# Retention with a recurrent state and a GELU feed-forward on one core: odd batches' heads swapped for 64x64 quarters, q and k loaded by rows and transposed by DMA

## The chip, the core and the metric

The kernel runs on one core of one Trainium2 chip. The metric is the device time of one execution in microseconds (us). The engines are named as the profile names them: PE (TensorE, matmuls), PEld (its weight loads), DVE (VectorE), ACT (ScalarE), POOL (GpSimd) and SP (SyncE, which here only issues DMAs).

## What is computed

```python
batch, n_heads, seq, head_dim = (4, 8, 768, 64)
gamma = 1.0 - 2.0 ** (-5.0 - np.arange(H))
for t in range(S):
    state = gamma * state + einsum('bhd,bhe->bhde', k[:, :, t], v[:, :, t])
    y[:, :, t] = scale * einsum('bhd,bhde->bhe', q[:, :, t], state)
x = y.transpose(0, 2, 1, 3).reshape(B * S, H * D)
h = x @ w_in                       # 3072 x 512 times 512 x 2048
g = 0.5 * h * (1 + tanh(c * (h + 0.044715 * h**3)))
out = g @ w_out                    # 3072 x 2048 times 2048 x 512
```

q, k, v and the output are float32.

## The kernel before

The sequence is cut into six chunks of 128 tokens (NCk = 6), and a chunk holds 128 tokens of all four batches, 512 rows. Within a chunk and a batch the recurrence becomes matmuls, in fp16:

- Transposed q and k (tile `qkT`, 128 partitions = two heads of 64): with two heads side by side on the partitions, there are four head pairs, `hp`.
- Scores, `mm_A` (L247, matmuls on L252): for each head pair and each of its heads j, k times q over 64 partitions, a 128x128 result. `ev_A` (L261, DVE on L265) multiplies them by a mask.
- State times q, `mm_yc` (L268, matmuls on L276): for each head, the 64x64 state times q. Head j sits on partitions 64j to 64j+63 of both operands and writes the same partitions of the result, so the two heads use two of the array's four 64x64 quarters.
- Scores times v, `mm_yi` (L285, L289), added into the same PSUM bank; `ev_Y` (L298) takes the sum to `xT`, the feed-forward's input.
- The state's update, `mm_s` (L307, L313) and `ev_S` (L321, L330).

The feed-forward of a chunk has two phases. `moe1` (L416; `moe1_two`, L422, in halves) multiplies `xT` by `w_in` on L398 in 16 units of d_ff and applies GELU on ACT (L414). `units_w` (L518) multiplies by `w_out` in 14 units of eight matmuls (L536) over a scheme of seven products instead of eight, which needs sums of GELU's results (`g_sums`, L476, on POOL until the last chunk, L467), three snapshots of partial results on ACT (L559) and a last copy (L565).

The order of the work is written by hand. `run(units, after)` (L597) issues the units of one chunk's feed-forward, and behind unit i the steps listed in `after[i]`: the preparation and the attention matmuls of the next chunk, and the loads and preparation of the one after it. Every engine and every DMA queue takes its instructions in that order. [...]

How q and k get into `qkT` before the change:

- Chunks 0 and 1: rows are loaded (`load1`, L100: 128 tokens x 8 heads x 64, 256 KB, in runs of 256 bytes), cast or scaled to fp16 (`prep1`, L184), transposed on PE against an identity (`mm_T`, L222, L229) and copied out of PSUM (`ev_T`, L234).
- Chunks 2 to 5, q, and chunks 3 to 5, k: `load_blk` (L106, issued on L113) loads them in 16 DMAs of 64 KB each, in runs of 128 bytes, so that head pairs and halves of a head already lie on the partitions; `prep_blk` (L201, L204) casts them; and VectorE's stream transpose, which works on blocks of 32x32, finishes the transpose (L238). k is loaded a second time by rows, for the state's update. Chunk 2's k goes by way of PE's transposes.
- `load(c)` (L117) issues a chunk's loads: chunk 2's is called ahead of chunk 1's feed-forward (L733), chunk 3's behind unit 8 of it (L746), and chunk c+2's behind unit 0 of chunk c (L798).

The stage between chunk 1's two phases is written on L734 to L769: chunk 2's q and k are prepared on ACT behind units 8, 9, 10 and 11 of `moe1` and units 0 and 1 of `units_w(1)`, chunk 2's first scores (batches 0 and 1) stand behind unit 14 and the others behind unit 4 of `units_w(1)`. From chunk 2 on the loop on L772 does the same with other unit numbers: scores of batches 0 and 1 of the next chunk behind unit 12, state times q behind units 19 and 25.

Of the kernel before, what the change touches and what calls it, by code (L numbers as in the profile page):

```python
# [9 lines left out]
F16 = mybir.dt.float16  # L10
# [6 lines left out]
def kernel(  # L17
# [30 lines left out]
    cst_np = np.concatenate([qdec, kdec, gst, tri], axis=1).astype(np.float32)  # L48
# [17 lines left out]
    OQ, OK, OG, OT = 0, H, 2 * H, 2 * H + NHP  # L66
# [12 lines left out]
    BLK = {"q": (2, 3, 4, 5), "k": (3, 4, 5)}  # L79

    def ld_all(key):
        if key not in raw:
            raw[key] = ld.tile(
                [128, B * NHP, 4, 32],
                F32,
                tag=key[0],
                bufs=2 if key[0] == "q32" else 1,
                name=key[0],
            )
        return raw[key]  # L90

    def ld_tile(nm, c, b):
        if nm == "q":
            t = ld_all(("q32", c)).rearrange("p (b hp) a d -> p b (hp a d)", b=B)
            return t[:, b].rearrange("p (h d) -> p h d", h=H)
        if (nm, c, b) not in raw:
            raw[nm, c, b] = ld.tile([128, H, Dh], F32, tag=f"{nm}32", bufs=8, name=f"{nm}32")
        return raw[nm, c, b]
# [7 lines left out]
    def load_blk(nm, c):  # L106
        t = ld_all((nm + ("32" if nm == "q" else "T32"), c))
        src = srcs[nm].rearrange("b (hp j) s (dd d) -> j dd s (b hp) d", j=2, dd=2)
        for j in range(2):
            for dd in range(2):  # L110
                for a in range(4):
                    p0, t0 = (2 * j + dd) * 32, c * C + a * 32
                    nc.sync.dma_start(  # L113
                        out=t[p0:p0 + 32, :, a, :], in_=src[j, dd, t0:t0 + 32]
                    )

    def load(c):  # L117
        load_blk("q", c)
        if c in BLK["k"]:
            for b in range(B):  # L120
                load1(nc.sync, "v", c, b)
            load_blk("k", c)
            for b in range(B):
                load1(nc.sync, "k", c, b)
        else:
            for b in range(B):
                for nm in "kv":
                    load1(nc.sync, nm, c, b)
# [32 lines left out]
    st = const.tile([128, B, NHP, 64], F16, name="st")  # L161
# [14 lines left out]
    blk16 = {}  # L176
# [6 lines left out]

    def prep1(eng, nm, c, b):  # L184
        t = pre.tile(
            [128, H, Dh], F16, tag=f"{nm}16", bufs=6 if nm == "q" else 2 * B, name=f"{nm}16"
        )
        src = ld_tile(nm, c, b)
        if (nm == "v") == (c < 2):
            copy_on(eng, t, src)  # L190
        else:
            col = OQ if nm == "q" else OK
            eng.tensor_tensor(  # L193
                out=t,
                in0=src,
                in1=cst[:, col:col + H].unsqueeze(2).broadcast_to([128, H, Dh]),
                op=ALU.mult,
            )
        h16[nm, c, b] = t

    def prep_blk(eng, nm, c, b):  # L201
        key, tag = ("q32", "q16") if nm == "q" else ("kT32", "kT16")
        t = pre.tile([128, NHP * 4, 32], F16, tag=tag, bufs=6 if nm == "q" else B, name=tag)
        copy_on(  # L204
            eng, t, ld_all((key, c))[:, b * NHP:(b + 1) * NHP].rearrange("p hp a d -> p (hp a) d")
        )
        blk16[nm, c, b] = t
# [14 lines left out]
    def mm_T(c, b):  # L222
        parts = [(i, nm) for i, nm in enumerate("qk") if c not in BLK[nm]]
        if not parts:
            return
        ps = bank("att", F16, (128, 2, NHP, 128), "qkT_ps")
        for i, nm in parts:
            for hp in range(NHP):
                nc.tensor.transpose(  # L229
                    out=ps[:, i, hp], in_=pair(h16[nm, c, b], hp), identity=iden  # L230
                )
        pss["T", c, b] = ps

    def ev_T(c, b, eng=nc.vector):  # L234
        t = att.tile([128, 2, NHP, 128], F16, tag="qkT", name="qkT")
        for i, nm in enumerate("qk"):
            if c in BLK[nm]:
                nc.vector.transpose(  # L238
                    out=t[:, i].rearrange("p hp t -> p (hp t)"),
                    in_=blk16.pop((nm, c, b)).rearrange("p ha d -> p (ha d)"),  # L240
                )
        if ("T", c, b) in pss:
            i0 = sum(c in BLK[nm] for nm in "qk")
            copy_on(eng, t[:, i0:], pss.pop(("T", c, b))[:, i0:])
        qkT[c, b] = t

    def mm_A(c, b):  # L247
        t = qkT[c, b]
        ps = [bank("att", name=f"a_ps{j}") for j in range(2)]
        for hp in range(NHP):  # L250
            for j in range(2):
                nc.tensor.matmul(  # L252
                    out=ps[j][:, hp],
                    lhsT=t[j * 64:(j + 1) * 64, 1, hp],
                    rhs=t[j * 64:(j + 1) * 64, 0, hp],
                    start=True,
                    stop=True,
                )
        pss["A", c, b] = ps

    def ev_A(c, b):  # L261
        ps = pss.pop(("A", c, b))
        for j in range(2):
            s = att.tile([128, NHP, 128], F16, tag=f"a{j}", name=f"a_sb{j}")
            nc.vector.tensor_tensor(out=s, in0=ps[j], in1=mask[:, j], op=ALU.mult)  # L265
            a_sb[c, b, j] = s

    def mm_yc(c, b, tag):  # L268
        y_ps = pss["Y", c, b] = bank(tag, name="y_ps")
        if c == 0:  # L270
            return

        for hp in range(NHP):
            for j in range(2):
                sl = slice(j * 64, (j + 1) * 64)
                nc.tensor.matmul(  # L276
                    out=y_ps[sl, hp],
                    lhsT=st[sl, b, hp],
                    rhs=qkT[c, b][sl, 0, hp],
                    start=(hp == 0),  # L280
                    stop=False,
                    skip_group_check=True,
                )
# [23 lines left out]
    def mm_s(c, bs, tag="att"):  # L307
# [3 lines left out]
        for i, b in enumerate(bs):  # L311
            for h in range(H):
                nc.tensor.matmul(  # L313
                    out=s_ps[h % 2 * 64:(h % 2 + 1) * 64, i, h // 2],
                    lhsT=h16["k", c, b][:, h],
                    rhs=h16["v", c, b][:, h],
                    start=True,
                    stop=True,
                )

    def ev_S(c, bs, eng=nc.vector):  # L321
# [3 lines left out]
        t = st[:, bs[0]:bs[-1] + 1]  # L325
        if c == 0:
            copy_on(eng, t, s_ps)
            return
        for hp in range(NHP):
# [3 lines left out]
                scalar=cst[:, OG + hp:OG + hp + 1],  # L333
# [14 lines left out]
    def att_AY(c, bs, tag, ca, abs_, eng):  # L348


        for b in bs:
            mm_yc(c, b, tag)
# [272 lines left out]
    mm_yc(0, 0, "o")  # L625
# [19 lines left out]
    mm_yc(0, 1, "o")  # L645
# [19 lines left out]
    mm_yc(0, 2, "o")  # L665
# [7 lines left out]
    mm_yc(0, 3, "o")  # L673
# [24 lines left out]
    def preps(c, b):  # L698
        prep1(VE, "q", c, b)
        prep1(PO, "k", c, b)  # L700
        prep1(AC, "v", c, b)

# [35 lines left out]
            for fp in range(NF // 2)  # L738
# [7 lines left out]
            8: [(prep_blk, AC, "q", 2, 0), (load, 3)],  # L746
            9: [(prep1, AC, "k", 2, 0)],
            10: [(att_T, 2, 0), (prep_blk, AC, "q", 2, 1)],
            11: [(prep1, AC, "k", 2, 1), (g_sums, PO, 1, 0, 4, 1, 2)],
            12: [(att_T, 2, 1)],  # L750
# [7 lines left out]
            0: [(prep_blk, AC, "q", 2, 2), (prep1, AC, "k", 2, 2)],  # L758
            1: [(att_T, 2, 2), (prep_blk, AC, "q", 2, 3), (prep1, AC, "k", 2, 3)],
            2: [(att_T, 2, 3)],  # L760
            4: [(att_AY, 2, (0, 1), "h", 2, (2, 3), AC)],
            9: [(att_AY, 2, (2, 3), "h", 2, (), AC), (mm_s, 2, (0, 1)), (mm_s, 2, (2, 3)),
                (ev_S, 2, (0, 1)), (ev_S, 2, (2, 3))],
            10: [(prep_blk, AC, "q", 3, 0)] + [(prep1, PO, "v", 3, b) for b in range(B)],
            11: [(prep_blk, AC, "q", 3, 1)],
            12: [(prep_blk, AC, "q", 3, 2)],
            13: [(prep_blk, AC, "q", 3, 3)],
# [4 lines left out]
    for c in range(2, NCk):  # L772
# [3 lines left out]
            15: [(att_T, n, 3)],  # L776
            16: [(prep1, AC, "k", n, 0), (prep1, AC, "k", n, 1)],
            17: [(prep1, AC, "k", n, 2), (prep1, AC, "k", n, 3)],
            19: [(att_AY, n, (0, 1), "h", n, (2, 3), VE)],
            25: [(att_AY, n, (2, 3), "h", n, (), AC), (mm_s, n, (0, 1)), (mm_s, n, (2, 3)),  # L780
                 (ev_S, n, (0, 1)), (ev_S, n, (2, 3))],
# [5 lines left out]
        if n < NCk:  # L787
            for b in range(B - 1):
                if c == 2:
                    more((8, 9, 11)[b], (prep_blk, AC, "k", n, b))  # L790
                more(((9, 10, 13) if c == 2 else (6, 8, 13))[b], (att_T, n, b))
            if c == 2:
                more(13, (prep_blk, AC, "k", n, 3))
# [3 lines left out]
        if m < NCk:  # L797
            more(0, (load, m))  # L798
            for b in range(B):
                more((20, 21, 23, 24)[b], (prep_blk, AC, "q", m, b))  # L800
                more(24, (prep1, PO, "v", m, b))
                more(29, (prep_blk, PO, "k", m, b))
# [31 lines left out]
```

## Time and profile before

| | us |
|---|---|
| median of 3 runs | 212.22 |
| the three runs | 210.81, 212.77, 212.22 |
| the profiled execution's time | 210.97 |
| its span, first to last instruction | 209.2 |
| PE busy | 200.5 |
| scores, L252: 192 matmuls, busy | 8.1 |
| state times q, L276: 160 matmuls, busy | 6.7 |
| PE transposes, L229: 80 matmuls, busy | 7.8 |
| DVE stream transposes, L238: 28, busy | 19.3 |
| ACT's waits for the feed-forward's first matmuls | 34.0 |

A chunk of the middle takes some 30 us: chunk 2's `moe1` starts at 88.08 and chunk 3's at 118.79. How to read it: busy times of PE count matmuls that overlap, so the chain of work, in order of time, is the better view of what a group costs. The granted TensorE clock is 1.00 throughout. DMA is the busy share of the 16 DMA engines; between 58 and 68 us it is above 1.00 by the profile's count, at 221 to 242 GB/s.

### The profile page before, as it was taken

The numbers are of one execution on the slowest core, as the hardware profiler recorded it, in microseconds if no ns is written. First come the engines' busy times: TensorE is split into PE (matmuls) and PEld (weight loads), VectorE is DVE, ScalarE is ACT, GpSimd is POOL, SyncE is SP. The second block draws the span as 40 slices with busy tenths as digits, with TensorE's granted clock in tenths as the row PEclk, the third lists the DMA queues.
The fourth block names the chain that finished last, engine by engine and source line by source line (L and its number), as shares of the span: only waits on it lengthen the run. The fifth ranks groups of instructions, "written<-read, shape, count | busy, mean of one in ns | idle before, by whom it ended". The sixth has DMA issues, their size and how long they took to land.

```text
span 209.2 us, 4776 instructions
## 1 busy us (share of the span) xinstructions
PE 200.5 (96%) x1928; PEld 132.2 (63%) x1928; DVE 103.8 (50%) x213; ACT 102.0 (49%) x182; POOL 115.6 (55%) x120
## 2 busy tenths in 40 slices
PE   7889999999998999999999999999999999999992
PEld 2447744456786878844688744688644788545881
DVE  3445144478733647803855730865632684053430
ACT  2483563154449625178745266633365811566311
POOL 0596001133089999249999299997499980200000
PEclk9999999999999999999999999999999999999999
DMA  7999999998899688699888798797960000500004
GB/s 167 285 257 207 206 206 222 273 252 227 166 205 244 106 159 174 105 292 216 125 193 147 124 350 139 146 200 109 236 197 0 0 3 0 204 0 0 0 28 177
DMA packets 124438, 33.19 MB, mean 159 GB/s; under 512 B 117952, under 2 KB 122432, under 8 KB 124416
## 3 DMA queue, kind: packets, MB, share of 16 engines
q1 hardware_dynamic: 108272, 21.09, 50.5%
q0 software_dynamic: 5456, 8.65, 17.6%
q10 hardware_dynamic: 10688, 3.15, 6.4%
q8 instruction: 15, 0.25, 0.4%
q14 instruction: 7, 0.06, 0.1%
HBM read 30.78 MB, written 6.29 MB: 177 GB/s over the span
## 4 chain that ended last, share of the span: by engine, by line
PE 90%; ACT 4%; DMA 2%; issue 1%; ACTq 0%; SPq 0%; DVE 0%
PE h_ps L398 39%; PE o_ps L536 29%; PE o_ps L432 7%; PE a_ps L252 3%; PE y_ps L289 3%; PE y_ps L276 3%; PE qkT_ps L229 2%; DMA iden<-rr_ident 2%; PE s_ps L313 2%; PE spin_ps L156 1%; ACT g L414 1%; ACT qkT L180 1%; ACT k L180 1%; ACT q L180 1%; ACTq L101 0%
## 5 line engine op out<-in xcount | busy, mean ns | idle before, releaser
L398 PE MATMUL h_ps<-xT,w_in 128*128 128x512 f16 (+2 forms) x488 | 87.4, 334 | 0.5 <-ACT g L414 0.5
L414 ACT ACTIVATE g<-h_ps 128x512 f16<-128x512 f32 (+1 forms) x98 | 57.5, 589 | 34.3 <-PE h_ps L398 34.0
L398 PEld LDWEIGHTS <-w_in 128*128 128x128 f16 x488 | 45.4, 97 | 37.4 <-issue 2.8
L467 POOL TENSOR_TENSOR s_g<-g 128x512 f16<-128x512 f16 x32 | 37.0, 1155 | 9.3 <-ACT g L414 9.3
L265 DVE TENSOR_TENSOR a_sb<-a_ps,mask 128x512 f16<-128x512 f32 x48 | 30.1, 683 | 22.9 <-PE a_ps L252 22.9
L536 PEld LDWEIGHTS <-s_g 128*128 128x128 f16 x320 | 30.5, 98 | 4.3
L536 PE MATMUL o_ps<-t_w,s_g 128*128 128x256 f16 x240 | 27.3, 273 | 0.0
L536 PEld LDWEIGHTS <-g 128*128 128x128 f16 x240 | 23.4, 98 | 3.5
L467 POOL TENSOR_TENSOR s_g<-s_g,g 128x512 f16<-128x512 f16 x16 | 18.5, 1156 | 1.3
L536 PE MATMUL o_ps<-w_out,g 128*128 128x256 f16 x160 | 18.6, 273 | 0.0
L467 POOL TENSOR_TENSOR s_g<-g,s_g 128x512 f16<-128x512 f16 x16 | 18.5, 1156 | 0.0
L193 POOL TENSOR_TENSOR k<-k,cst 128x512 f16<-128x512 f32 x8 | 8.4, 1053 | 17.4 <-DMA k<-in_k_dram 17.4
L569 POOL DMA_DIRECT2D out_dram<-o_sb x8 | 5.9, 739 | 19.6 <-DVE o_sb L467 18.1
L193 POOL TENSOR_TENSOR v<-v,cst 128x512 f16<-128x512 f32 x16 | 16.2, 1044 | 0.0
L565 ACT COPY o_sb<-o_ps 128x512 f32<-128x512 f32 (+1 forms) x5 | 2.7, 543 | 25.3 <-PE o_ps L536 25.3
L432 PE MATMUL o_ps<-w_out,g 128*128 128x512 f16 x64 | 14.8, 379 | 0.0
L238 DVE STREAM_TRANSPOSE qkT<-kT 128x512 f16<-128x512 f16 x12 | 8.2, 679 | 12.9 <-ACT kT L180 8.9
L305 DVE TENSOR_TENSOR xT<-y_ps,dec 128x512 f16<-128x512 f32 x16 | 10.3, 686 | 4.5 <-PE y_ps L289 4.5
L238 DVE STREAM_TRANSPOSE qkT<-q 128x512 f16<-128x512 f16 x16 | 11.1, 691 | 2.6 <-ACT q L180 2.5
L559 ACT COPY s_u<-o_ps 128x512 f32<-128x512 f32 (+1 forms) x6 | 3.1, 515 | 17.4 <-PE o_ps L536 10.6
L156 PE MATMUL spin_ps<-zero 128*128 128x512 f16 x32 | 9.9, 447 | 1.2 <-DVE zero L148 1.2
L330 DVE SCALAR_TENSOR_TENSOR st<-st,cst,s_ps 128x128 f16<-128x128 f16 (+1 forms) x40 | 9.9, 315 | 2.0 <-PE s_ps L313 2.0
(55 smaller groups left out, 184.7 us busy)
## 6 DMA issues: line engine op xcount, KB each, us to landing
k<-in_k_dram SPq DMA_DIRECT2D x22, 256.0 KB, 4.3
v<-in_v_dram SPq DMA_DIRECT2D x18, 256.0 KB, 4.5
q<-in_q_dram SPq DMA_DIRECT2D x64, 64.0 KB, 2.9
out_dram<-o_sb POOLq DMA_DIRECT2D x8, 512.0 KB, 4.4
kT<-in_k_dram SPq DMA_DIRECT2D x48, 64.0 KB, 2.8
w_in<-in_moe_w_in_dram POOLq DMA_DIRECT2D x4, 512.0 KB, 8.9
w_out<-in_moe_w_out_dram POOLq DMA_DIRECT2D x4, 512.0 KB, 14.8
v<-in_v_dram ACTq DMA_DIRECT2D x6, 256.0 KB, 5.6
```

The costliest lines, as they stand in the source:

```text
L156: nc.tensor.matmul(out=ps, lhsT=zero[:, 0:128], rhs=zero, start=True, stop=True)
L180: eng.copy(out=out, in_=in_)
L193: eng.tensor_tensor(out=t, in0=src, in1=cst[:, col:col + H].unsqueeze(2).broadcast_to([128, H, Dh]), op=ALU.mult,)
L238: nc.vector.transpose(out=t[:, i].rearrange("p hp t -> p (hp t)"), in_=blk16.pop((nm, c, b)).rearrange("p ha d -> p (ha d)"),)
L265: nc.vector.tensor_tensor(out=s, in0=ps[j], in1=mask[:, j], op=ALU.mult)
L305: nc.vector.tensor_tensor(out=x, in0=ps, in1=dec, op=ALU.mult)
L330: nc.vector.scalar_tensor_tensor(out=t[:, :, hp], in0=t[:, :, hp], scalar=cst[:, OG + hp:OG + hp + 1], in1=s_ps[:, :, hp], op0=ALU.mult, o ...
L398: nc.tensor.matmul(out=out, lhsT=w_in_sb[wi][:, kc, wr * 128:(wr + 1) * 128], rhs=xT[c][:, kc, t0:t1], start=(kc == 0), stop=(kc == NHP - ...
L414: nc.scalar.activation(out=out, in_=in_, func=AF.Gelu_apprx_tanh, scale=1.0)
L432: nc.tensor.matmul(out=ps[:, n0:n1], lhsT=g_sb[c, fc // 8][:, fc % 8, b * C:(b + 1) * C], rhs=w_out_sb[fc // (NF // NO)][:, fc % (NF // NO ...
L467: eng.tensor_tensor(out=out, in0=in0, in1=in1, op=op)
L536: nc.tensor.matmul(out=po, lhsT=lhs(c, lk, fp, a), rhs=rhs(rk, fp), start=(new and fp == 0 and (last or a == 0)), stop=(stop and fp == NP ...
```

## The change

Four things are changed together.

1. In odd batches the two heads of each pair are swapped where q and k are prepared (`heads`), so head j sits on partitions of the other half. The state of odd batches is kept in that order too (`st` is split by parity, a second set of decay columns `gst_o`), `mm_s` takes v of the other head, and `ev_A` picks the other PSUM bank.
2. `mm_yc` takes the batches of a step together: for each head pair it issues two batches times two heads, and these four matmuls lie on the four 64x64 quarters of the array.
3. `mm_A` computes each 128x128 score in two halves of 64 rows: 16 matmuls of 64x64 weights per batch instead of 8 of 64x128.
4. Chunks 2 to 5 load q, k and v by rows only (`load`: twelve DMAs of 256 KB), cast q and k on ACT into one tile `qk16`, and one DMA on SP's queue, `dma_T`, transposes the tile (128 x 1024, fp16) into `qkT`. `load_blk`, `prep_blk`, the stream transposes and PE's transposes of chunk 2's k are gone. The preparation of chunk n moves into the `units_w` phase two chunks earlier in full; `qkT` has 6 buffers instead of 4.

The core of the diff:

```diff
     def load(c):
-        load_blk("q", c)
-        if c in BLK["k"]:
...
+        for b in range(B):
+            load1(nc.sync, "q", c, b)
+            load1(nc.sync, "k", c, b)
+        for b in range(B):
+            load1(nc.sync, "v", c, b)
...
+    def heads(ap, b):
+        v = ap.rearrange("p (hp j) d -> p hp j d", j=2)
+        return v[:, :, ::-1] if b % 2 else v
...
+    def dma_T(c, b):
+        nc.sync.dma_start_transpose(
+            out=qkT_tile(c, b).rearrange("p i hp t -> p (i hp) t"),
+            in_=qk16.pop((c, b)).rearrange("p i h d -> p (i h d)"),
+        )
...
     def mm_A(c, b):
         t = qkT[c, b]
         ps = [bank("att", name=f"a_ps{j}") for j in range(2)]
         for hp in range(NHP):
-            for j in range(2):
...
+            for m in range(2):
+                for j in range(2):
+                    nc.tensor.matmul(
+                        out=ps[j][m * 64:(m + 1) * 64, hp],
+                        lhsT=t[j * 64:(j + 1) * 64, 1, hp, m * 64:(m + 1) * 64],
+                        rhs=t[j * 64:(j + 1) * 64, 0, hp],
...
+    def mm_yc(c, bs, tag):
...
         for hp in range(NHP):
+            for b in bs:
+                for j in range(2):
+                    r = j ^ b % 2
+                    sl = slice(r * 64, (r + 1) * 64)
+                    nc.tensor.matmul(
+                        out=pss["Y", c, b][j * 64:(j + 1) * 64, hp],
+                        lhsT=st_of(b)[sl, hp],
+                        rhs=qkT[c, b][sl, 0, hp],
...
+    def preps2(c, b):
+        prep1(AC, "q", c, b)
+        prep1(AC, "k", c, b)
+        dma_T(c, b)
...
-            8: [(prep_blk, AC, "q", 2, 0), (load, 3)],
-            9: [(prep1, AC, "k", 2, 0)],
-            10: [(att_T, 2, 0), (prep_blk, AC, "q", 2, 1)],
-            11: [(prep1, AC, "k", 2, 1), (g_sums, PO, 1, 0, 4, 1, 2)],
-            12: [(att_T, 2, 1)],
+            8: [(prep1, AC, "q", 2, 0), (load, 3)],
+            9: [(prep1, AC, "k", 2, 0), (dma_T, 2, 0)],
+            10: [(prep1, AC, "q", 2, 1)],
+            11: [(prep1, AC, "k", 2, 1), (dma_T, 2, 1), (g_sums, PO, 1, 0, 4, 1, 2)],
...
-            0: [(prep_blk, AC, "q", 2, 2), (prep1, AC, "k", 2, 2)],
-            1: [(att_T, 2, 2), (prep_blk, AC, "q", 2, 3), (prep1, AC, "k", 2, 3)],
-            2: [(att_T, 2, 3)],
+            0: [(prep1, AC, "q", 2, 2), (prep1, AC, "k", 2, 2), (dma_T, 2, 2)],
+            1: [(prep1, AC, "q", 2, 3), (prep1, AC, "k", 2, 3), (dma_T, 2, 3)],
...
-            10: [(prep_blk, AC, "q", 3, 0)] + [(prep1, PO, "v", 3, b) for b in range(B)],
-            11: [(prep_blk, AC, "q", 3, 1)],
-            12: [(prep_blk, AC, "q", 3, 2)],
-            13: [(prep_blk, AC, "q", 3, 3)],
+            10: [(preps2, 3, 0)],
+            11: [(preps2, 3, 1)],
+            12: [(preps2, 3, 2)],
+            13: [(preps2, 3, 3)] + [(prep1, PO, "v", 3, b) for b in range(B)],
...
-            15: [(att_T, n, 3)],
-            16: [(prep1, AC, "k", n, 0), (prep1, AC, "k", n, 1)],
-            17: [(prep1, AC, "k", n, 2), (prep1, AC, "k", n, 3)],
...
-                more((20, 21, 23, 24)[b], (prep_blk, AC, "q", m, b))
+                more((20, 21, 23, 24)[b], (prep1, AC, "q", m, b))
+                more((21, 23, 24, 26)[b], (prep1, AC, "k", m, b), (dma_T, m, b))
                 more(24, (prep1, PO, "v", m, b))
-                more(29, (prep_blk, PO, "k", m, b))
```

## The prediction

> **What bounds the kernel now.** I read the page's busy shares and its chain of work first, then the chain in order of time around the places that the diff touches, then SyncE's own list of DMA issues, and last GpSimd's order in chunk 2.
>
> ```profile
> span 209.2 us, 4776 instructions
> PE 200.5 (96%) x1928; PEld 132.2 (63%) x1928; DVE 103.8 (50%) x213; ACT 102.0 (49%) x182; POOL 115.6 (55%) x120
> ...
> PE 90%; ACT 4%; DMA 2%; issue 1%; ACTq 0%; SPq 0%; DVE 0%
> ```
>
> TensorE is the bound: 90% of the chain is its matmuls. So what leaves VectorE, ScalarE or GpSimd gains nothing by itself; what counts is TensorE's instructions and whatever makes it wait.
>
> ```profile
> 64.38 0.51 ACT k L180
> 64.90 0.05 issue
> 64.94 0.40 PE qkT_ps L229 x4
> ...
> 69.55 0.55 PE a_ps L252 x16
> 70.11 0.98 PE h_ps L398 x8
> 71.09 1.76 PE o_ps L536 x16
> ...
> 76.69 0.56 PE y_ps L276 x16
> 77.26 0.55 PE a_ps L252 x16
> ...
> 88.08 11.69 PE h_ps L398 x52
> ...
> 145.06 0.51 PE s_ps L313 x32
> ```
>
> Columns: start, length, piece. To be seen: 16 matmuls of state times q (L276) and 16 of the scores (L252) cost 0.55 us each; the stage from 63 to 75 is the one where ScalarE's copies of q and k hold TensorE up; and 32 small matmuls of L313, each with its own weight load, take 0.51 us, 16 ns each.
>
> ```profile
> 46.48 1.50 SPq L732 DMA_DIRECT2D dec<-rr_dec  x1
> 48.07 9.48 SPq L113 DMA_DIRECT2D q<-in_q_dram  x16
> 57.59 0.49 SPq L101 DMA_DIRECT2D k<-in_k_dram  x1
> ...
> 65.03 10.06 SPq L113 DMA_DIRECT2D q<-in_q_dram  x16
> ...
> 133.07 3.12 SPq L101 DMA_DIRECT2D v<-in_v_dram  x4
> ```
>
> SyncE issues chunk 2's loads from 48.07 and goes straight on to chunk 3's at 65.03. It is never idle here: the DMA engines set its pace. The eight row loads (256 KB) from 57.59 to 65.03 took 7.44 us, 0.93 us each.
>
> ```profile
> k<-in_k_dram SPq DMA_DIRECT2D x22, 256.0 KB, 4.3
> out_dram<-o_sb ACTq DMA_DIRECT2D x2, 256.0 KB, 2.0
> ```
>
> From issue to landing, 256 KB took 4.3 us in the busy queue and 2.0 us (the last stores) in an idle one.
>
> **Part 1: chunk 2's first transposes (path).** Chunks 2 to 5 no longer use VectorE's 28 stream transposes (0.69 us each, beside TensorE, worth nothing on the path) nor TensorE's 16 transposes of chunk 2's k. In their place stand 16 DMA transposes of 256 KB on SyncE. The order is what costs: chunk 3's twelve loads are emitted at unit 8, the first transpose at unit 9, so on SyncE the first transpose stands behind all 24 row loads of chunks 2 and 3. From 48.07, 24 x 0.93 = 22.3, so it issues at 70.4. No row shows a DMA transpose; the nearest is the 256 KB row load in the same queue. With its 4.3 the first lands at 74.7, the second 0.93 later, at 75.6, and its half of the scores (0.28) ends at 75.9. TensorE would be there at about 68.2: without its own transposes the stage follows ScalarE's GELUs and copies, 0.50 each, from 63.27 on. The scores now end at 70.11, so this is +5.8 us. Low end: loads at 0.78 (3.12/4), landing 2.0: scores end at 69.9, -0.2. High end: loads at 1.09 (the four at 104.04 took 4.37), a transpose at the pace of 128-byte packets (9.48/4 = 2.37 per 256 KB) and the longest landing of a q load (7.1): 84.0, +13.9. I take +5.8, since the queue is full by the rows.
>
> **Part 2: chunk 2's other transposes (path).** From 71.09 to the end of the next scores (77.81) is 6.72 us. After: five units of 0.88, state times q 0.34 and scores 0.55 would be 5.3. But ScalarE does GELU 0.5, two copies, the snapshot (after the second unit, 1.8 to 2.4) and two copies, so the last transpose issues at 3.4; with 3.2 to landing (middle of 2.0 and 4.3) and 0.28 of scores it ends at 6.9: +0.2. Ends: -1.0 (landing 2.0) and +4.1 (7.1).
>
> **Part 3: a slow restart of TensorE after the wait.** The wait in part 1 would be some 6 us; the longest of the trace while matmuls run is 0.7. A row on restarts: at the start 14 spin matmuls ran from 1.19 to 6.01, 4.82 us; later six take 1.40, so 14 would take 3.27: 1.6 us lost from a cold start, though the granted clock reads 1.00 in that stretch. Between 0 and +1.6 I take the middle, +0.8. The Trainium skill (TensorE: Matmul & The Clock Gate, Part 1) says that the array's clock drops to half after an idle window of about 3.4 us and comes back after as long a busy one. By that rule the term would be +1.6 rather than +0.8; no trace here shows a drop behind a wait.
>
> **Part 4: the end of chunk 1's output, and GpSimd.** The copies of chunk 3's q and k now run on ScalarE in units 10 to 13: one copy more (0.5) stands ahead of chunk 2's first GELU, while the four kT copies leave that stage (11.69 against 11.35 in the next chunk): +0.2, between -0.3 and +0.5. GpSimd's four v products (4.05) move from ahead of chunk 1's two stores to behind them: its queue is 89.73 + 4.05 = 93.8 when it can start the sums that began at 92.38. The sum that TensorE takes at 108.86 was done at 108.49, so 0.4 is slack; 1.4 late and TensorE some 0.2 later gives +0.8, between 0 and +1.4. Later chunks have their kT casts (2.29) gone and lose nothing.
>
> **Part 5: quarters (path).** State times q of two batches: 16 matmuls over two quarters take 0.56, 8 take 0.34, so 0.22 is the streaming of four more per quarter. Four quarters at once: 0.34 for 16. Part 2 holds one such group; seven are left: -1.5, or 0 if they don't overlap. Scores: twice the matmuls over four quarters, the same streaming. L313's 16 ns shows that issuing is no limit at 32 x 16 = 0.51, so 0. If all cost what a matmul costs now (27.5 ns), 192 more cost +5.3. Where scores follow state times q the array's shape no longer changes; a group's edge is 0.56 - 16 x 0.0275 = 0.12, six places: -0.2, between -0.7 and 0.
>
> **Part 6: covered.** The other twelve transposes issue one stage or more before their scores (chunk 3's from about 83 on, wanted at 99.78) and cost nothing; without that cover each would show its landing, 2.0 to 7.1. ScalarE now waits, before chunk 4's third copy, for a buffer that chunk 3's state matmuls free; four copies queue behind it, about 2.1 us, against four units of 3.5: nothing. Chunk 4's loads go behind chunk 3's last transpose, at about 91, and need 11.2 before about 108: nothing.
>
> **Sum.** 5.8 + 0.2 + 0.8 + 0.2 + 0.8 - 1.5 - 0.2 = +6.1. The profiled execution took 210.97 us (span 209.2, the rest around it unchanged): 217.1. The median of the runs shown, 212.22, is 1.25 above that execution, so I forecast 218.3. All low ends: -3.7, 208.5; all high ends: +26.8, 239.0.
>
> **Rivals.**
> Faster, the transposes come in time. The place is TensorE's arrival at 68.2, the price is part 1. Landed by then, part 1 is -1.4, part 2 -1.0, part 3 nothing: sum -3.1, 209.1. It decides if the second transpose has landed by about 69.4, which needs loads of 0.78 and a landing of 2.0. Chunk 5's four v loads ran at 0.78; the eight rows of this very stretch, at 0.93, speak against it.
> No change: the second lands by 72.4 (loads at 0.85, landing under 3), the wait is short and the restart warm; the quarters pay for it: about 212.
> Transposes that are dear: if one keeps the queue 2.37 us and lands after 7.1, part 1 is 70.4 + 2.37 + 7.1 + 0.28 - 70.11 = +10.0, part 2 +4.5, part 3 +1.6 and the rest -0.7: +15.4, about 228. For it: packets of 128 bytes ran at a third of the rows' pace; against it: source and target are both on the chip. The Trainium skill (VectorE: DVE Perf Modes, The three transpose paths) gives 1309 ns for a 128x128 transpose by DMA; eight in a row would be an estimated 10.5 us each, the queue would never empty, and the time would be over 260 us. No row bears on it.
> Quarters that do not overlap (the change does not do what it says): parts 1 to 4 and up to +5.3 without the -1.5: about 222 at half of that. The 16 ns of L313 speak against it.
>
> **How the numbers follow.** Late transposes 0.52, no change 0.17, faster 0.13, dear 0.10, no overlap 0.08. A measurement of this kernel can tell about 1% (2.1 us) from no change. Faster 0.13, within 1% 0.17, slower 0.52 + 0.10 + 0.08 = 0.70. The range 210.5 to 225.0 leaves out most of the faster case and half of the dear one; the likeliest case alone reaches from 214.3 to 224.
>
> **What would show it.** Part 1: a wait of TensorE at chunk 2's first scores put down to a DMA, and SyncE's first transpose issued near 70. Part 2: a shorter wait about 5 us later. Part 3: matmuls at nearly twice their spacing behind the first wait, with the granted clock down. Part 4: GpSimd's sums ending after TensorE asks for them in chunk 2. Part 5: 16 matmuls of state times q in 0.34, 32 of the scores in 0.55. I am wrong if TensorE passes chunk 2's first scores before 70, or if it waits for transposes in chunks 3 to 5.

## The result

| | us |
|---|---|
| before, median of 4 runs beside it | 212.5 (210.81 to 212.98) |
| after, median of 4 runs | 223.1 (222.78 to 223.91) |
| ratio | 1.052, 95% interval 1.045 to 1.059 |
| profiled execution after: time, span | 223.91, 222.1 |
| profiled execution before: time, span | 210.97, 209.2 |

The change makes the kernel 5.2% slower. The forecast was 218.3, range 210.5 to 225.0: the sign and the mechanism came out as forecast, the size did not. The sum of the steps was +6.1 us. Between the medians it is +10.6, and between the two profiled executions, whose traces are read below, +12.9: the one of before lies 1.5 below its median and the one of after 0.8 above.

### The profile page after: what moved, and what is told of

Read it like the earlier page. It is cut to its first block, busy times and chain, and to the rows that moved or that the text cites. A ratio compares the mean times of both kernels' runs of the same rounds, so it can differ in the third digit from the quotient of the medians.

```text
span 222.1 us, 4990 instructions
## 1 busy us (share of the span) xinstructions
PE 200.5 (90%) x2104; PEld 131.8 (59%) x2104; DVE 84.8 (38%) x181; ACT 100.4 (45%) x178; POOL 111.1 (50%) x112
## 4 chain that ended last, share of the span: by engine, by line
PE 54%; POOL 25%; DMA 8%; issue 6%; SPq 3%; ACT 1%; ACTq 0%; DVE 0%; POOLq 0%
PE h_ps L377 25%; POOL s_g L446 22%; PE o_ps L515 17%; PE o_ps L411 6%; DMA w_in<-in_moe_w_in_dram 4%; DMA k<-in_k_dram 3%; POOL v L173 3%; PE y_ps L267 2%; SPq L86 2%; ACT g L393 1%; DMA qkT<-qk 1%; PE a_ps L225 1%; PE s_ps L291 1%; PE y_ps L254 1%; SPq L213 1%
## 5 line engine op out<-in xcount | busy, mean ns | idle before, releaser
L377 PE MATMUL h_ps<-xT,w_in 128*128 128x512 f16 (+2 forms) x488 | 88.1, 336 | 2.1 <-DMA w_in<-in_moe_w_in_dram 1.1
L377 PEld LDWEIGHTS <-w_in 128*128 128x128 f16 x488 | 45.9, 98 | 39.5 <-issue 2.9
L515 PEld LDWEIGHTS <-s_g 128*128 128x128 f16 x320 | 30.4, 98 | 6.1 <-POOL s_g L446 2.2
L515 PE MATMUL o_ps<-t_w,s_g 128*128 128x256 f16 x240 | 27.7, 273 | 1.4 <-POOL s_g L446 1.4
L515 PEld LDWEIGHTS <-g 128*128 128x128 f16 x240 | 24.1, 100 | 4.2
L225 PE MATMUL a_ps<-qkT 64*64 64x128 f16 x384 | 9.7, 226 | 12.3 <-DMA qkT<-qk 11.9
L515 PE MATMUL o_ps<-w_out,g 128*128 128x256 f16 x160 | 19.4, 282 | 0.0
L225 PEld LDWEIGHTS <-qkT 64*64 64x64 f16 x384 | 6.8, 110 | 15.9 <-DMA qkT<-qk 12.6
L124 PE MATMUL spin_ps<-zero 128*128 128x512 f16 x32 | 10.8, 483 | 1.2 <-DVE zero L116 1.2
L283 DVE TENSOR_TENSOR xT<-y_ps,dec 128x512 f16<-128x512 f32 x16 | 10.3, 686 | 3.9 <-PE y_ps L267 3.9
L148 ACT CAST qk<-q 128x512 f16<-128x512 f32 x16 | 9.9, 618 | 2.9 <-issue 1.7
```

What stands on the lines that cost most here:

```text
L124: nc.tensor.matmul(out=ps, lhsT=zero[:, 0:128], rhs=zero, start=True, stop=True)
L148: eng.copy(out=out, in_=in_)
L225: nc.tensor.matmul(out=ps[j][m * 64:(m + 1) * 64, hp], lhsT=t[j * 64:(j + 1) * 64, 1, hp, m * 64:(m + 1) * 64], rhs=t[j * 64:(j + 1) * 64, ...
L283: nc.vector.tensor_tensor(out=x, in0=ps, in1=dec, op=ALU.mult)
L377: nc.tensor.matmul(out=out, lhsT=w_in_sb[wi][:, kc, wr * 128:(wr + 1) * 128], rhs=xT[c][:, kc, t0:t1], start=(kc == 0), stop=(kc == NHP - ...
L515: nc.tensor.matmul(out=po, lhsT=lhs(c, lk, fp, a), rhs=rhs(rk, fp), start=(new and fp == 0 and (last or a == 0)), stop=(stop and fp == NP ...
```

## The profile after

First the page's top: span, busy times, the slices of TensorE, its granted clock and the DMA engines, and the chain's shares by engine.

```profile
span 222.1 us, 4990 instructions
PE 200.5 (90%) x2104; PEld 131.8 (59%) x2104; DVE 84.8 (38%) x181; ACT 100.4 (45%) x178; POOL 111.1 (50%) x112
PE   7887999999995059799999899999999999999993
PEclk9999999999999558999999999999999999999999
DMA  7999999999799952247998259990590000220004
...
PE 54%; POOL 25%; DMA 8%; issue 6%; SPq 3%; ACT 1%; ACTq 0%; DVE 0%; POOLq 0%
```

TensorE's busy time is 200.5 us, as before, in a span that is 12.9 longer. The hole is one place: the 5, 0, 5 in the PE row (slices of 5.55 us, so these are 66.6 to 83.3 us). The clock is at half in the second and third of them and not back in the slice behind. GpSimd, which the chain of before did not hold at all, is 25% of this one. That share is not a loss: all of TensorE's waits for GpSimd's sums come to 1.4 us.

SyncE's DMA issues (start, length, what):

```profile
47.02 0.57 SPq L86 DMA_DIRECT2D q<-in_q_dram  x1
...
71.83 3.82 SPq L86 DMA_DIRECT2D v<-in_v_dram  x4
75.76 28.18 SPq L213 DMA_TRANSPOSE qkT<-qk  x8
```

24 row loads go out from 47.02 to 75.7 without a pause, 1.19 us each, and the first transpose stands behind the last of them. Line 213 is the transpose; its first one was issued at 75.76.

TensorE in the same stretch (start, length to the end of the last matmul, what, and in brackets the idle time before it and who ended it):

```profile
65.81 3.73 PE L377 MATMUL h_ps<-xT,w_in 128*128 128x256 f16 x29
79.86 0.64 PE L225 MATMUL a_ps<-qkT 64*64 64x128 f16 x16 [10.33 <-DMA qkT<-qk]
80.79 0.64 PE L225 MATMUL a_ps<-qkT 64*64 64x128 f16 x16 [0.28 <-DMA qkT<-qk]
81.36 1.89 PE L377 MATMUL h_ps<-xT,w_in 128*128 128x256 f16 x8
83.04 4.74 PE L515 MATMUL o_ps<-w_out,g 128*128 128x256 f16 x32
...
90.49 0.42 PE L225 MATMUL a_ps<-qkT 64*64 64x128 f16 x16 [1.26 <-DMA qkT<-qk]
```

TensorE stands for 10.33 us at chunk 2's first scores. Behind the wait, eight matmuls of L377 take 1.89 us and 32 of L515 take 4.74; the same eight took 1.05 before the change, and the 32 of L515 take 3.66 at full clock (in the kernel with spin matmuls, below). The granted clock says why (columns: stretch, its length, busy time and instructions of PE, PEld, DVE, ACT and POOL, then the clock, the DMA share and GB/s):

```profile
71.00:71.50 0.50, 0.00 (x0) 0.00 (x0) 0.00 (x0) 0.00 (x0) 0.50 (x1) 1.00 1.22 276
71.50:72.00 0.50, 0.00 (x0) 0.00 (x0) 0.00 (x0) 0.00 (x0) 0.50 (x2) 0.59 1.00 226
...
85.00:85.50 0.50, 0.50 (x5) 0.42 (x4) 0.00 (x0) 0.00 (x0) 0.42 (x2) 0.76 0.00 0
85.50:86.00 0.50, 0.50 (x7) 0.44 (x6) 0.00 (x0) 0.00 (x0) 0.50 (x1) 1.00 0.00 0
```

Between these stretches the clock is 0.50. A mean of 0.59 places the fall from 1.00 to 0.50 at 71.59, 2.05 us after the last matmul (69.54); the 0.76 places the return at 85.24, 4.4 us after the matmuls took up again for good (80.79).

Last the chain of work in chunk 2's feed-forward, in order of time:

```profile
121.57 1.17 POOL s_g L446
122.74 0.05 issue
122.78 4.76 PE o_ps L515 x42
127.54 0.35 PE y_ps L254 x16
127.89 0.57 PE y_ps L267 x16
128.46 0.50 PE s_ps L291 x32
```

State times q over four quarters takes 0.35 for 16 (0.56 before). But what leads to it now is GpSimd: its last sum but two of this chunk ends at 122.7, and TensorE waited 1.03 for it.

Where the 12.9 us came from, by the start of the same piece of work in both profiles:

| piece | before | after | later by | added in between |
|---|---|---|---|---|
| chunk 0, first matmul of `moe1` | 16.87 | 18.26 | 1.4 | 1.4 |
| chunk 2, end of the first scores | 70.11 | 81.43 | 11.3 | 9.9 |
| chunk 2, `moe1` | 88.08 | 100.96 | 12.9 | 1.6 |
| chunk 3, `moe1` | 118.79 | 132.56 | 13.8 | 0.9 |
| chunk 4, `moe1` | 149.17 | 162.73 | 13.6 | -0.2 |
| chunk 5, `moe1` | 179.06 | 192.38 | 13.3 | -0.2 |
| end of the last matmul | 205.24 | 218.56 | 13.3 | 0.0 |

The last stores end 0.4 us sooner behind the last matmul, which gives the 12.9.

## The experiments

Each ratio is against the kernel before on the same chip in the same session, with a 95% interval. The names in the expectations are those of the headings.

### e1_load3_behind: chunk 3's loads behind chunk 2's transposes

```diff
-            8: [(prep1, AC, "q", 2, 0), (load, 3)],
+            8: [(prep1, AC, "q", 2, 0)],
...
-            1: [(prep1, AC, "q", 2, 3), (prep1, AC, "k", 2, 3), (dma_T, 2, 3)],
+            1: [(prep1, AC, "q", 2, 3), (prep1, AC, "k", 2, 3), (dma_T, 2, 3), (load, 3)],
```

> Chunk 3's twelve row loads are issued behind chunk 2's four transposes instead of ahead of them; nothing else changes. Theory (place in SyncE's queue): the 10.3 us wait at chunk 2's first scores goes, and the stretch at half clock behind it (about 2 us) with it; the second wait (1.3 us) stays at most: about 210 to 211, near the kernel before. Rival (the DMA transposes themselves are dear, wherever they stand): a wait of several us stays at chunk 2's scores and the time stays above 216.

211.62 us (12 runs), ratio 1.000 (0.997 to 1.003). SyncE and the chain of work:

```profile
64.91 10.89 SPq L213 DMA_TRANSPOSE qkT<-qk  x4
```

```profile
66.92 2.78 DMA qkT<-qk
69.70 0.04 issue
69.75 0.42 PE a_ps L225 x16
...
74.57 2.73 DMA qkT<-qk
77.30 0.04 issue
77.35 0.42 PE a_ps L225 x16
```

One call moved, twelve loads, and 11.0 us come back by the ratios (1.052 to 1.000), as the theory expected. Chunk 2's transposes take 1.23 to 1.33 us of SyncE's time each and 2.7 to 2.8 us to landing. So the loss was the place in SyncE's queue, not the price of a transpose. What is left are waits of 0.92 and 1.26 us for transposes, and 1.72 and 0.2 for GpSimd's sums, and the time is 0.6 above the theory's 210 to 211.

### e2_spin_in_wait: the wait filled with 44 spin matmuls

```diff
-            14: [(att_AY, 1, (), "o", 2, (0, 1), None), (prep1, PO, "v", 2, 0), (prep1, PO, "v", 2, 1)],
+            14: [(spin, 44), (att_AY, 1, (), "o", 2, (0, 1), None), (prep1, PO, "v", 2, 0), (prep1, PO, "v", 2, 1)],
```

> 44 dummy matmuls of 128x512 (9.5 us at full clock) are put ahead of chunk 2's first scores, so TensorE is busy during most of the wait; everything else as in the changed kernel. Theory (the idle time drops the clock): the granted clock stays at full speed and the time falls by about 2 us, to 221. Rival (the low clock behind the wait is hidden by the next transposes): the clock stays up and the time stays at 223.

221.15 us (6 runs), ratio 1.044 (1.040 to 1.048). TensorE:

```profile
69.30 9.66 PE L124 MATMUL spin_ps<-zero 128*128 128x512 f16 x44
79.15 0.42 PE L225 MATMUL a_ps<-qkT 64*64 64x128 f16 x16 [0.19 <-DMA qkT<-qk]
80.11 0.42 PE L225 MATMUL a_ps<-qkT 64*64 64x128 f16 x16 [0.54 <-DMA qkT<-qk]
80.45 1.05 PE L377 MATMUL h_ps<-xT,w_in 128*128 128x256 f16 x8
81.34 3.66 PE L515 MATMUL o_ps<-w_out,g 128*128 128x256 f16 x32
```

Useless matmuls make the kernel faster than the changed one, by what the theory expected: the transposes come about as late, but the clock stays up. The 40 matmuls behind the scores take 4.38 us to the start of the next group (80.45 to 84.83) instead of 6.26 (81.36 to 87.62), so the slow restart is worth 1.9 us by these rows. The ratios say 1.6 (1.0519 less 1.0443, times 212), with an uncertainty as large.

### e11_transposes_on_act: the transposes on another queue

```diff
-        nc.sync.dma_start_transpose(
+        (nc.scalar if c == 2 else nc.sync).dma_start_transpose(
```

> The changed kernel with chunk 2's four transposes issued on ScalarE's DMA queue instead of SyncE's; chunk 3's loads stay where they are. My theory: the place behind the 24 loads on SyncE is what made the transposes late, so on another queue they issue behind their copies at about 65 to 67 and land, with the DMA engines full of loads, 4 to 6 us later: TensorE waits 1 to 3 us instead of 10.3, its clock stays up, and ScalarE loses some time to the issues: 212 to 216. Rival: the DMA engines are what is full, and a transpose on any queue lands only when the loads have: 219 to 223, as the changed kernel.

216.92 us (6 runs), ratio 1.023 (1.019 to 1.027): 6.1 us come back by the ratios, a little less than I expected. ScalarE, and TensorE's waits:

```profile
65.99 1.32 ACTq L213 DMA_TRANSPOSE qkT<-qk  x1
67.36 0.60 ACT L393 ACTIVATE g<-h_ps 128x512 f16<-128x512 f32 x1 [1.40 <-PE h_ps L377]
```

```profile
PE h_ps L377 <- ACT g L393: 3.8, 5, 1.5
PE a_ps L225 <- DMA qkT<-qk: 3.4, 3, 1.6
```

The first transpose issues right behind its copy, at 65.99 instead of 75.76, though chunk 3's loads run on SyncE all the while. It takes 1.32 us of ScalarE, ahead of a GELU that TensorE waits for: 3.8 us of such waits (1.0 in the changed kernel). The first two land 5.27 and 4.68 us after their issue beside the loads, against 2.80 and 2.78 in e1. So the queue's order is most of the loss; the full DMA engines are the smaller part, and the issuing engine pays for the way round.

### e3_two_quarters: state times q batch by batch

e1 with the two loops of `mm_yc` exchanged:

```diff
-        for hp in range(NHP):
-            for b in bs:
+        for b in bs:
+            for hp in range(NHP):
```

> As the run with chunk 3's loads behind, but state times q goes batch by batch, so that two neighbouring matmuls use two quarters instead of four. Theory: each of the eight groups of 16 takes 0.56 instead of 0.35 us; those ahead of GpSimd's sums in chunks 3 and 4 are partly hidden by the wait for the sums: 0.8 to 1.7 us slower than that run. Rival (the quarters are worth nothing, the order of issue does not matter): no difference.

213.44 us (6 runs from 210.83 to 215.23), ratio 1.011 (1.006 to 1.016). This experiment failed: in its profile (an execution of 210.83) a group of L254 takes about what it does in e1, the next group following 0.24 to 0.37 behind its start against 0.25 to 0.35. With the heads still swapped, the two batches together use all four quarters whatever the order, which is probably why nothing was undone. The six runs spread over 4.4 us, and three of them (210.83, 212.49, 212.86) lie within 1% of the kernel before, so the timed 1% is no sign of an effect.

### e4_v_products_early: GpSimd's v products ahead of its stores

e1 with chunk 3's four v products emitted at unit 10 instead of 13:

```diff
-            10: [(preps2, 3, 0)],
+            10: [(preps2, 3, 0)] + [(prep1, PO, "v", 3, b) for b in range(B)],
...
-            13: [(preps2, 3, 3)] + [(prep1, PO, "v", 3, b) for b in range(B)],
+            13: [(preps2, 3, 3)],
```

> As the run with chunk 3's loads behind, and GpSimd's four v products of chunk 3 stand ahead of chunk 1's stores again. Theory: GpSimd's sums of chunk 2 start on time, TensorE's wait for them in chunk 2 (1.0 us) goes: 0.8 us faster than that run. Rival (the sums are late for another reason): no difference.

211.62 us (12 runs), ratio 1.000 (0.997 to 1.002): nothing. The products now wait 8.0 us for v itself, whose loads had been put behind the transposes, and the sums start at 94.44 (94.20 in e1). My expectation missed that e1 had moved their input.

### e5_reliefs: the waits that are left taken away

```diff
-            8: [(prep1, AC, "q", 2, 0), (load, 3)],
-            9: [(prep1, AC, "k", 2, 0), (dma_T, 2, 0)],
...
+            4: [(att_AY, 1, (3,), "o", 1, (), VE), (prep1, AC, "q", 2, 0)],
+            5: [(prep1, AC, "k", 2, 0), (dma_T, 2, 0)],
...
+            11: [(prep1, AC, "k", 2, 3), (dma_T, 2, 3), (load, 3), (g_sums, PO, 1, 0, 4, 1, 2)],
...
-            13: [(preps2, 3, 3)] + [(prep1, PO, "v", 3, b) for b in range(B)],
+            13: [(preps2, 3, 3)] + [(prep1, VE, "v", 3, b) for b in range(B)],
...
-            after[at] = [(g_sums, PO if n < NCk else VE, c, 2 * i, 2 * i + 2)] + after.get(at, [])
+            after[at] = [(g_sums, PO if n < NCk and i < 3 else VE, c, 2 * i, 2 * i + 2)] + after.get(at, [])
```

> The changed kernel with three moves. Chunk 2's copies and transposes go to units 4 to 11 of chunk 1's first feed-forward phase (chunk 3's loads behind them, and nothing of chunk 2 is left in units 0 and 1 of the second phase); chunk 3's four v products go from GpSimd to VectorE; and in chunks 2 to 4 the last of the four groups of sums goes from GpSimd to VectorE. My theory: what is left in the kernel with the loads moved is TensorE's waits for the two transposes (0.92 and 1.26 us) and for GpSimd's sums (1.72 in chunk 2, less in the two chunks behind). If those are the only things that hide the quarters' gain, 211.6 less some 3.5 to 4.5 us: 207 to 208. Rival 1: the waits go but others come in their place (copies on ScalarE now stand ahead of GELUs in chunk 1, VectorE's sums late): 210 to 212. Rival 2: the quarters bring nothing and only the waits count: 208.5 to 209.5.

206.98 us (4 runs from 206.49 to 207.03; before 211.02), ratio 0.979 (0.976 to 0.982): 2.1% faster than the kernel before, and just under the forecast of the first theory. The chain in chunk 3:

```profile
116.40 11.35 PE h_ps L377 x52
127.75 0.57 PE a_ps L225 x32
128.32 2.70 PE h_ps L377 x12
131.02 3.49 PE o_ps L515 x32
134.51 0.35 PE y_ps L254 x16
```

After 30 us TensorE waits once, 0.5 us for a GELU; neither a transpose nor GpSimd holds it up any more.

### e6_heads_unswapped and e7_scores_64x128: the two halves of the quarters

e6 is e5 with the heads of odd batches in their old order:

```diff
-        return v[:, :, ::-1] if b % 2 else v
+        return v
...
-                    r = j ^ b % 2
+                    r = j
```

(and the matching index in `mm_s`, `ev_A` and `ev_S`); e7 is e5 with `mm_A` as before the change.

> The kernel of e5_reliefs with the heads of odd batches not swapped: state times q of both batches of a step lies on the same two quarters, all else stays. My theory: a group of 16 such matmuls goes back from 0.35 to 0.56 us, eight groups of 0.21: 1.7 us more than e5_reliefs, 0.8 per cent, and visible in the chain because no wait of GpSimd follows any more. Rival: the four quarters are worth nothing on the path: equal to e5_reliefs within 0.3 us.

> The kernel of e5_reliefs with the scores as before the change: 8 matmuls of 64x128 weights per batch instead of 16 of 64x64. My theory: the halves stream as fast, 16 against 32 matmuls both take 0.55 us, so 0 to +0.5 us against e5_reliefs (the array's shape changes again at six places, 0.1 each at most). Rival: twice the matmuls cost issue and weight loads: faster than e5_reliefs by up to 2 us.

e6: 208.70 us (4 runs), ratio 0.987 (0.984 to 0.991), 1.7 us more than e5 in the same session. Its chain:

```profile
129.46 2.69 PE h_ps L377 x12
132.16 3.49 PE o_ps L515 x32
...
142.58 0.56 PE y_ps L254 x16
```

0.56 instead of 0.35, as before the change; chunk 3 takes 30.27 us from `moe1` to `moe1` (117.54 to 147.81), in e5 29.84 (116.40 to 146.24). The swap is worth its 1.7 us when nothing absorbs it.

But e6 is still 2.3 us faster than the kernel before, so the swap is not all of e5's gain. From chunk 0's first matmul of `moe1` to chunk 2's the kernel before takes 71.2 us (16.87 to 88.08) and e6 68.6 (18.08 to 86.71); in chunks 2 to 4 the two differ by 0.2 a chunk at most. In that stretch the kernel before has TensorE's transposes of chunk 2's k, four groups with 0.23 us each to the next group's start, and TensorE waits there for ScalarE's copies of k. Together they are 2.2 of the 2.6. The waits (who waited for whom: us in total, times, longest):

```profile
PE qkT_ps L229 <- ACT k L180: 1.3, 3, 0.5
```

e7: 207.54 us (4 runs), ratio 0.982 (0.979 to 0.986), 0.6 more than e5, with intervals that overlap. 16 large scores take 0.55, 32 small ones 0.57; behind state times q the small ones take 0.45. So the halved scores cost nothing, and perhaps save a few tenths by keeping the array's shape.

### e10_load3_unswapped: the same undo where GpSimd is still waited for

e1 with the edit of e6.

> The kernel of e1_load3_behind (chunk 3's loads behind chunk 2's transposes, GpSimd as in the changed kernel) with the heads of odd batches not swapped: state times q back on two quarters. In e6_heads_unswapped, where nothing waits for GpSimd, this cost 1.7 us. My theory: in e1_load3_behind TensorE waits for GpSimd's sums by 1.72 us in chunk 2 and less in the next two, so what TensorE loses ahead of those waits is taken from them: 0.3 to 1.0 us slower than e1_load3_behind. Rival: the sums' wait does not absorb it, 1.7 us slower.

212.86 us (12 runs), ratio 1.004 (1.001 to 1.006) against e1's 1.000 of another session: some 0.8 us, with an uncertainty as large. The profiles are clearer: chunk 3 takes 30.36 us against e1's 30.12, chunk 4 29.85 against 29.63, so 0.23 a chunk where e5 and e6 differ by 0.43. In these two chunks about half of the swap's gain is lost in the wait for the sums. Chunk 2 can't be compared so: in e10's profile, whose execution took 214.95, its wait for the sums is longer than in e1, 2.49 against 1.72, and the clock falls behind it.

### e9_before_sums: the kernel before with e5's move of the sums

```diff
-            after[at] = [(g_sums, PO if n < NCk else VE, c, 2 * i, 2 * i + 2)] + after.get(at, [])
+            after[at] = [(g_sums, PO if n < NCk and i < 3 else VE, c, 2 * i, 2 * i + 2)] + after.get(at, [])
```

> A control: the kernel before with one of the three moves of e5_reliefs, the last of the four groups of sums on VectorE instead of GpSimd in chunks 2 to 4. In the kernel before the sums end 0.4 us ahead of their first use and GpSimd is not in the chain of work, so my theory expects no gain: 0 to -0.3 us, or a small loss since VectorE is 50 per cent busy there with the stream transposes. Rival: the sums hold TensorE up by amounts that the profile does not show, and e5_reliefs owes its gain to this move and not to the change: 1 us faster or more.

217.02 us (6 runs), ratio 1.025 (1.020 to 1.029): 5 us slower, where I had expected about nothing. VectorE and TensorE in chunk 3:

```profile
135.81 1.26 DVE L467 TENSOR_TENSOR s_g<-s_g,g 128x512 f16<-128x512 f16 x1
137.00 1.37 DVE L467 TENSOR_TENSOR s_g<-g 128x512 f16<-128x512 f16 x1
138.29 1.26 DVE L467 TENSOR_TENSOR s_g<-g,s_g 128x512 f16<-128x512 f16 x1
139.47 0.70 DVE L238 STREAM_TRANSPOSE qkT<-q 128x512 f16<-128x512 f16 x1
```

```profile
138.33 0.40 PE L252 MATMUL a_ps<-qkT 64*128 64x128 f16 x8
140.82 0.40 PE L252 MATMUL a_ps<-qkT 64*128 64x128 f16 x8 [2.09 <-DVE qkT L238]
141.72 7.08 PE L536 MATMUL o_ps<-t_w,s_g 128*128 128x256 f16 x48
```

```profile
141.00:142.00 1.00, 1.00 (x26) 0.73 (x21) 0.73 (x2) 0.00 (x0) 1.00 (x2) 0.94 0.70 109
145.00:146.00 1.00, 1.00 (x9) 0.87 (x8) 0.28 (x1) 0.72 (x2) 0.00 (x0) 0.86 0.88 144
```

The sums stand ahead of the last batch's stream transposes on VectorE; TensorE waits 2.09 us for them (4.3 in chunks 2 to 4 together), and behind that wait the clock is at 0.50 from 141.9 to 145.3, so 48 matmuls take 7.08 where the same 48 took 5.42 in chunk 2. The move is a loss in the kernel before, where stream transposes stand behind it; in e5, which has none, VectorE's sums hold nothing up. So the transposes by DMA bring two things: room on VectorE for GpSimd's work, and, as e6 shows, TensorE's time at chunk 2's k.

### e8_before_again: the start

> The kernel before, once more: how much the start varies from one execution to another. In the profiled executions so far the first feed-forward matmul of chunk 0 began at 16.87 us (before) and at 17.3 to 18.3 (the kernels with the change), where all wait for w_in's load, which the change doesn't touch. If the start varies by itself, this run begins it somewhere between 16.9 and 18.3; if the change causes it, at 16.9 again.

210.68 us; the first matmul of `moe1` at 16.77. The three profiles of kernels with the old code have it at 16.77 to 16.87 (e9 16.85), the ten with the new code at 17.31 to 18.28. So the changed program does start 0.5 to 1.4 us later. In the profile after, one of the latest, TensorE waits 1.1 us for the first part of w_in: issued at 9.05 (9.02 before), it lands 9.2 us later. The kernel before has no such wait, so my premise that all wait for w_in was wrong. Undoing the swap does not bring it back (e6 18.08, e10 17.36). Which part of the change does it stays open.

## Why the prediction came out as it did

Part 1, the place behind 24 loads: right in every step but the pace. "24 x 0.93 = 22.3" took the pace of the eight row loads at the end of the stretch for all 24; they took 28.7 us, 1.19 each, chunk 2's twelve 16.4 and chunk 3's twelve 12.1, with the DMA engines moving 242 GB/s. The 0.93 was a pace of issues that the engines did not keep: 256 KB in 0.93 us is 282 GB/s, and in that stretch they moved 221 to 242. At those rates 256 KB take 1.08 to 1.19 us and 24 loads 26 to 28.5, so the rates already known would have given nearly the right term. The issue came at 75.76 instead of 70.4, although the first load went out a microsecond sooner (47.02). The rest held: the first tile 4.1 us after its issue (4.3), and TensorE ready at 69.5 (68.2, plus the start's 1.4). That the second came 0.93 behind the first, as forecast, was luck: it was issued 2.09 later (77.85) and landed in 2.89. So the term was 9.9 instead of 5.8. It lies within the part's ends (-0.2 to +13.9), but the pace alone does not: 1.09 a load was taken as its worst.

Part 2: +0.2 forecast; at full clock, in e1, the stretch from the first scores to the second is 7.59 against 7.70, so -0.1.

Part 3, "the middle, +0.8": mis-sized; it measured 1.9 by the rows. (The longest wait of the kernel before while matmuls run is 0.8, not 0.7.) Its own high end, the 1.6 of the row on restarts, was the better guide: the profile of before counts six spin matmuls from 2.00 to 4.00 us and six from 5.00 to 6.00, half the pace at first, though its clock column reads 1.00 for both. So was the Trainium skill (TensorE: Matmul & The Clock Gate, Part 1), by which an idle window of some 3.4 us halves the clock and as long a busy one brings it back. The trace agrees on the halving, and the time at 0.50 lasted 13.65 us here and 3.4 in e9, four windows and one. It differs from the page's warning against gaps over 3.4 us: the clock fell 2.05 us after the last matmul here, and a gap of 2.09 us was enough in e9. The page calls the window free-running, but that alone doesn't explain it, since a gap of 2.09 can't fill a window of 3.4: the 3.41 us ahead of the fall held 1.36 us of matmuls here (68.18 to 69.54) and 1.3 in e9, so in these runs a window that lowers the clock was not wholly idle.

Part 4: chunk 2's first GELUs +0.2 forecast, 0.22 measured (11.91 against 11.69); GpSimd's sums +0.8 forecast, a wait of 1.03 measured. "Later chunks ... lose nothing" holds for GpSimd alone: in chunk 3 its last sum but two ends 20.3 us behind the start of `moe1` in both kernels (139.12 less 118.79, and 152.90 less 132.56). But the prediction had no term for that end as a bound on TensorE, which now comes earlier by the quarters and waits 0.2 for it in chunks 3 and 4 each.

Part 5: a group of 16 in 0.35 (0.34 forecast), 32 scores in 0.57 (0.55). The whole came to 1.7 in e5 against e6, over eight groups (1.5 over seven forecast). In the changed kernel only 0.2 a chunk arrived in chunks 3 and 4, because the wait for GpSimd's sums took the other half: the step that failed here is the sum of the groups on their own, 0.22 each.

Part 6: right. TensorE waits for a transpose three times in all, each in chunk 2.

Not in the sum: the start, +1.4 in the profiled execution.

The sum again, as measured: start 1.4, part 1 9.9, parts 2 and 3 with the first two groups of quarters 1.6, the rest of chunk 2 0.9, chunks 3 and 4 -0.4, the last stores -0.4: 13.0, against 12.9 between the spans. Of the 6.8 that the forecast of +6.1 lacked, 4.1 are the loads' pace, 1.4 the start and 1.1 the clock; the other 0.2 is what is left of smaller terms that cancel, the quarters' missing half against the last stores and part 2. By the medians it lacked 4.5.

The rivals. Faster, if the transposes come in time: e1 met nearly that condition and stood at 211.6, since waits of 0.92, 1.26 and 1.72 were left; e5 met it in full, with GpSimd's waits gone too, at 207.0. Its price for parts 1 and 2, -2.4 together, was about right: e6, without the swap, is 2.6 shorter up to chunk 2's `moe1`. Dear transposes: false for those that TensorE waits for. They took 1.2 to 2.0 us of the queue each, 2.7 to 2.8 us to landing with no loads around and 2.9 to 5.3 beside loads. Dear ones exist, but off the path: in e1 one of chunk 3's held SyncE for 3.17 us and landed after 7.7. The estimate of 10.5 us for eight, scaled from the Trainium skill's 1309 ns for a 128x128 transpose (VectorE: DVE Perf Modes, The three transpose paths), is not borne out; a single transpose of that size is in no run here. No overlap of quarters: false, by e6.

## What to carry to other kernels

A DMA's price is first its place in its queue: count all that is issued ahead of it, at the pace of the whole stretch and not of its best part, before looking at what the transfer itself costs. A wait of TensorE of 2 us or more can cost its own length and then 1.4 to 1.9 us more at half clock (1.9 here, 1.7 in e9, 1.4 in e10). A saving on TensorE arrives only as far as the engine that it waits for next lets it: the swap's 1.7 us came in full only when part of GpSimd's sums had moved to VectorE, which the change had freed. In this kernel the loads' place alone cost as much as the whole 5.2% loss; with earlier transposes and that move besides it became a 2.1% gain.

## What the runs showed of the hardware beyond that

- A DMA transpose of 128 x 1024 fp16 values (256 KB) within the chip cost about what a row load of 256 KB does: mostly 1.24 us of its queue and 2.7 to 2.8 us to landing, beside other traffic up to 3.17 and 7.7 (e1).
- Issued from ScalarE, it held that engine for 1.25 to 1.32 us.
- The clock fell behind gaps of TensorE of 10.3 us, 2.49 (in e10's profile, 0.50 around 113) and 2.09; in e1, with gaps of 1.72 and 1.26, it stayed at 1.00. The idle time in a fixed window fits these traces better than the length of the gap: divided into windows of 3.41 us, counted from the clock's own changes, each of these three falls stands at the end of a window with 1.99 to 2.09 us idle, and the windows at full clock with 1.51 us idle or less brought none (1.51 is e1's, whose gap of 1.72 lies across a window's edge). Nothing between 1.51 and 1.99 occurred.
- In e9 a sum of fp16 tiles took VectorE 0.41 us once GpSimd's sums had ended, and mostly 1.19 to 1.38 beside GpSimd's work (the first of a group 0.43 and 0.70); GpSimd's went from 1.16 to 1.35. What they contend for was not tried.
